# Part B with dense projections, its heads moved to 32-row groups through DRAM, and its instructions in an order laid down by hand

## The chip, the cores and the metric

The kernel runs on one core of one Trainium2 chip, in one launch. The metric is the device time of a run in microseconds; the time before is the median of three runs.

## What is computed

`x` has 2048 tokens of width 640. Part A is a recurrent attention over 64 segments of 32 tokens with 8 memory rows carried from segment to segment; the change does not touch its code. Part B is an attention of 32 heads of 20 numbers each, in which a token looks at itself and seven earlier tokens two apart. A gate mixes both.

```python
def _B_ref(x, wqkv, wo):
    B, S, D = x.shape
    H = 32
    Dh = D // H
    W, dil = (8, 2)
...
    logits = jnp.einsum('bhsd,bhswd->bhsw', q, kg) * scale
    logits = jnp.where(mask[None, None, :, :], logits, -1000000000.0)
    attn = _softmax(logits, axis=-1)
    o = jnp.einsum('bhsw,bhswd->bhsd', attn, vg)
    return (lambda x, *d: x.transpose(*d))(o, 0, 2, 1, 3).reshape(B, S, D) @ wo
x = A_x
g = _sigmoid((x * gate_w).sum(-1, keepdims=True))
a = _A_ref(x, A_mem0, A_Wq, A_Wk, A_Wv, A_Wo, A_seg_len)
b = _B_ref(x, B_wqkv, B_wo)
return g * a + (1 - g) * b
```

## The kernel before

The program has three stages in time. **Part B** (`part_b`, L90 to L331) computes the gate and all of Part B, writes (1 - g) * b to a DRAM scratch, and stores x, transposed, for Part A. **The prepass** (`prepass`, L422) projects the last 8 tokens of every segment with Part A's Q, K and V weights. **Part A** (`part_a`, L519) runs the 64 segments.

Part A's weights are cut into 80 slices of 384 KB (`slice_keys`, L333). 14 are streamed again in every segment, the others stay in SBUF. Of those, N_EARLY = 23 are loaded while Part B runs, and with them the 20 slices of Part A's output weight are copied within DRAM into a contiguous scratch, `wscr` (`load_early`, L377). Another 27 are loaded when Part B's SBUF is given back (`load_late(0)`), and 16 later.

Part B works on five blocks of tokens: four of 484 (`BQ` = 4 x 121) and one of 112. In a block the queries are split by parity of the position into units of 121 (`nu` = 4 of them), so that a unit's eight keys lie in a band of 128 consecutive rows. `steps` (L292) lists (block b, group g of 4 heads), 8 groups a block. The weights of Q, K and the output are padded: every head of 20 columns stands in 32 (`wqk`, L125; `wop`, L124), so a group of 4 heads fills 128 rows and each head starts at a multiple of 32, where the small matmuls of `scores` and `values` need it. The padding costs memsets on POOL and copies on DVE and POOL at the start (L130, L135, L138).

For each step the code calls, in this order, `proj` of the next step (L219: 2 chains of 5 matmuls, one for Q and one for K, with DVE copying Q and ACT copying K out of PSUM), `scores` (L234: 16 matmuls, two exponentials on ACT, two multiplications by the band mask on DVE), `values` of the step before (L256: 16 matmuls for the sums, 16 for the outputs, then logarithm and exponential on ACT for the reciprocal, L271 and L272, and the normalization on DVE, L274), and, from block 1 on, one `out_tile` (L277: 2 chains of 8 matmuls on 128 tokens, scaled by ACT and DVE, stored from ACT's queue). Once a block there are `make_xT` (L159: 20 transposes, the gate, the copies to `xh_blk` on POOL and their store) at g = 2 and `make_v` (L201: 8 chains of 5 matmuls) at g = 6. The order on each engine in Part B is chosen by the scheduler from this program order and its estimates; nothing is fixed by hand there. In Part A the order on PE, ACT and DVE is written by hand (L556).

PSUM has 8 banks: two for all chains (`psm`, L108), four for scores (`psS`, two tiles of two banks), one each for outputs and sums (`psO`).

DMAs of weights, of `xh_blk` and of small things go on SP's queue, those of x and of the outputs on ACT's. Two `issue_after` edges fix an order on SP: `load_early` and the streamed loads of the prepass come after the first store of `xh_blk` (L297, L916).

## Time and profile before

| what | us |
|---|---|
| median of three runs | 1759.74 (1759.62 to 1760.73) |
| the profiled execution's own time | 1748.09 |
| its span, first to last instruction | 1746.1 |
| Part B, to the prepass's first matmul | 0 to 225.4 |
| prepass, to Part A's first matmul | 225.4 to 385.5 |
| Part A | 385.5 to 1746.0 |

Over the span PE is busy 95%, ACT 50%, DVE 37%, POOL 4%. DMA moves 466.5 MB. The granted TensorE clock is 0.998. The profile's chain of waits lists what ended last, step by step; a busy share is an average over three stages that have different limits, so the stages are read one by one. The time of one execution lies between the first and the last instruction's marks, its span, plus about 2 us around it.

### The profile page before, as it was taken

The page shows a single profiled execution, that of the slowest core. Times are in us where ns is not written, and L with a number is a line of the kernel's source. Part 1 is how long each engine was busy: PE and PEld are TensorE (multiplying, and loading weights), DVE is VectorE, ACT ScalarE, POOL GpSimd, SP SyncE. Part 2 cuts the span into 40 slices and gives each one's busy share as a digit, 9 for nine tenths or more (in the row PEclk, how much of TensorE's full clock was granted, in tenths as well). Part 3 has the DMA queues.
Part 4 walks back from the last instruction along what each step waited for, and adds up shares of the span by engine and source line. Part 5 has one row for each costly group of instructions (what it writes and reads, how often), then busy time and mean ns, then how long its engine had stood idle before and what let it go on. Part 6 is the DMA issues. An engine that isn't in the chain of part 4 may idle for free.

```text
span 1746.1 us, 82407 instructions
## 1 busy us (share of the span) xinstructions
PE 1666.4 (95%) x36527; PEld 994.9 (57%) x36527; DVE 649.4 (37%) x2065; ACT 868.5 (50%) x2377; POOL 69.9 (4%) x132
## 2 busy tenths in 40 slices
PE   6899999999999999999999999999999999999989
PEld 3555544445556555556555555555555555555557
DVE  4565533223333333333333333333333333333330
ACT  3776632224555555555555555555555545555550
POOL 4011000000000000000000000000000000000000
PEclk9999999999999999999999999999999999999999
DMA  6951184899999999999999999999999989999981
GB/s 172 335 133 27 42 303 113 221 275 309 307 299 304 298 309 299 305 301 308 295 302 302 299 300 300 302 298 307 303 297 305 298 295 300 306 302 298 300 288 30
DMA packets 280648, 466.50 MB, mean 267 GB/s; under 512 B 94820, under 2 KB 155748, under 8 KB 280292
## 3 DMA queue, kind: packets, MB, share of 16 engines
q1 hardware_dynamic: 178632, 401.83, 69.6%
q10 hardware_dynamic: 101660, 59.41, 11.7%
q8 instruction: 285, 4.67, 1.1%
q14 instruction: 71, 0.58, 0.1%
HBM read 427.47 MB, written 41.55 MB: 269 GB/s over the span
## 4 chain that ended last, share of the span: by engine, by line
PE 86%; ACT 7%; issue 2%; DMA 2%; DVE 2%; ACTq 1%; DVEq 0%
PE ps_qk L569 26%; PE ps_v L662 13%; PE ps_wo L726 12%; PE ps_qkT L586 6%; PE ps_pre L442 6%; PE ps_S L616 5%; PE ps_oT L685 3%; PE ps_z L883 3%; PE ps_bqk L226 3%; ACT bP L249 2%; PE ps_pre L454 2%; ACT ZB L810 2%; PE ps_mem L736 1%; PE ps_bv L213 1%; PE ps_S L625 1%
## 5 line engine op out<-in xcount | busy, mean ns | idle before, releaser
L578 ACT CAST TZ<-ps_qk 128x384 bf16<-128x384 f32 x448 | 208.2, 479 | 326.2 <-PE ps_qk L569 180.4
L569 PEld LDWEIGHTS <-hT 128*32 128x32 bf16 x10240 | 246.5, 96 | 150.0 <-DVE hT L739 13.2
L593 DVE COPY ZB<-ps_qkT 128x384 bf16<-128x384 bf16 x256 | 91.6, 358 | 377.6 <-PE ps_qkT L586 211.7
L569 PE MATMUL ps_qk<-wres_q,hT 128*32 128x384 bf16 x4096 | 225.8, 327 | 1.8 <-issue 1.5
L662 PE MATMUL ps_v<-wlate_v,hT 128*32 128x384 bf16 x4096 | 224.6, 329 | 0.0
L726 PEld LDWEIGHTS <-TZ 128*32 128x32 bf16 x6144 | 153.6, 96 | 65.8 <-issue 18.0
L569 PE MATMUL ps_qk<-wlate_k,hT 128*32 128x384 bf16 x2560 | 159.7, 328 | 0.0
L569 PE MATMUL ps_qk<-wst,hT 128*32 128x384 bf16 x1792 | 153.2, 328 | 0.3 <-issue 0.2
L662 PEld LDWEIGHTS <-hT 128*32 128x32 bf16 x5120 | 113.6, 96 | 68.9 <-issue 6.2
L726 PE MATMUL ps_wo<-wlate_oa,TZ 128*32 128x384 bf16 x2560 | 139.2, 327 | 2.3 <-issue 2.3
L616 PE MATMUL ps_S<-ZB,TZ 128*128 128x160 bf16 (+1 forms) x1024 | 136.9, 238 | 0.4 <-issue 0.4
L586 PE MATMUL ps_qkT<-ident,TZ 128*128 128x128 bf16 x1536 | 130.2, 221 | 0.2 <-issue 0.2
L726 PE MATMUL ps_wo<-wlate_ob,TZ 128*32 128x256 bf16 x2688 | 123.2, 275 | 7.4 <-issue 7.3
L586 PEld LDWEIGHTS <-TZ 128*128 128x128 bf16 x1536 | 89.1, 98 | 61.3 <-issue 40.8
L569 PE MATMUL ps_qk<-wres_k,hT 128*32 128x384 bf16 x1792 | 120.3, 328 | 1.2 <-issue 0.6
L634 ACT ACTIVATE ZB<-ps_S 32x224 bf16<-32x224 f32 x256 | 89.0, 348 | 41.7 <-PE ps_S L625 38.1
L696 DVE CAST TZ<-ps_oT 128x192 bf16<-128x192 f32 x256 | 79.4, 351 | 63.6 <-PE ps_oT L690 63.6
L696 ACT CAST TZ<-ps_oT 128x192 bf16<-128x192 f32 x256 | 69.7, 327 | 57.7 <-PE ps_oT L690 57.7
L616 PEld LDWEIGHTS <-TZ 128*128 128x128 bf16 (+1 forms) x1024 | 58.9, 95 | 68.4 <-issue 41.0
L739 DVE CAST hT<-ps_mem 128x24 bf16<-128x24 f32 x126 | 22.6, 179 | 195.7 <-PE ps_mem L736 195.7
L669 ACT CAST TZ<-ps_v 128x384 bf16<-128x384 f32 x192 | 92.3, 481 | 3.2
L546 POOL COPY TZ<-ZB 128x384 bf16<-128x384 bf16 x64 | 32.5, 507 | 1495.9 <-DMA ZB<-zpk_dram 582.5
(142 smaller groups left out, 2431.2 us busy)
## 6 DMA issues: line engine op xcount, KB each, us to landing
wst<-in_A_Wq_dram SPq DMA_DIRECT2D x260, 384.0 KB
wst<-in_A_Wv_dram SPq DMA_DIRECT2D x260, 384.0 KB
wst<-in_A_Wk_dram SPq DMA_DIRECT2D x195, 384.0 KB
wst<-wscr SPq DMA_DIRECT2D x192, 384.0 KB
zpk_dram<-ZS ACTq DMA_DIRECT2D x4, 3072.0 KB
ZB<-zpk_dram ACTq DMA_DIRECT2D x64, 192.0 KB
wscr<-in_A_Wo_dram SPq DMA_DIRECT2D x20, 384.0 KB
wres_q<-in_A_Wq_dram SPq DMA_DIRECT2D x16, 384.0 KB
```

What stands on the lines that cost most here:

```text
L226: nc.tensor.matmul(ps[:, 0:nn], lhsT=wqk[n][:, kc, 4 * g:4 * g + 4, :].rearrange("p h d -> p (h d)"), rhs=xT[:, kc, o0:o0 + nn], start=(kc ...
L442: nc.tensor.matmul(ps[:], lhsT=sls[r][kc][:, c0:c0 + 128], rhs=zTi[:, kc, :], start=(kc == 0), stop=(kc == KC - 1))
L569: nc.tensor.matmul(pq[32 * j:32 * j + 32, 0:384], lhsT=hT[:, kc, :], rhs=sl[:, 384 * j:384 * j + 384], start=(kc == 0), stop=(kc == KC - 1 ...
L578: cp(sts[i], pqs[i][:, 0:384])
L586: nc.tensor.transpose(pT[:, t, :, :, :].rearrange("p j b i -> p (j b i)"), st[:, 128 * t:128 * t + 128], self.ident[:])
L593: nc.vector.tensor_copy(q_blocks(R)[:, 1:5, :, :].rearrange("p b c i -> p c b i"), pT.rearrange("p t j b i -> p (t j) b i"))
L616: nc.tensor.matmul(grid(h, par)[:, :, 0:80].rearrange("p j (b r i) -> p j b r i", r=2, i=8)[:, :, :, r, :], lhsT=KT[k0:k1, 12 * r + c:12 * ...
L634: nc.scalar.activation(E[ps], pSs[h][ps, :, 112 * j:112 * j + 112], ACT.Exp, scale=scale_a)
L662: nc.tensor.matmul(pvs[R][32 * j:32 * j + 32, 0:384], lhsT=hT[:, kc, :], rhs=sl[:, 384 * j:384 * j + 384], start=(kc == 0), stop=(kc == KC ...
L669: cp(V[R], pvs[R][:, 0:384])
L696: cps[j % 2](oTxs[2 * h + j // 2][:, 6 * (j % 2):6 * (j % 2) + 6, :], pos[j][:, 0:240].rearrange("p (c q) -> p c q", q=40)[:, :, 8:40])
L726: nc.tensor.matmul(pso[part][32 * jj:32 * jj + 32, 0:n], lhsT=oTxs[2 * (R // 2) + j // 2][:, 6 * (j % 2) + 3 * (R % 2) + t, :], rhs=o_weig ...
```

## The change

Part B's work is the same; how it is laid out differs.

- The padded weights go. Q, K and the output weight are loaded as they are (`b_wq`, `b_wk`, `b_wo`), straight into their tiles from SP's and ACT's queues. A projection chunk `f` is 128 dense columns, so a block has 5 chunks for Q and 5 for K in place of 8 groups each. An output tile has 2 chains of 5 matmuls in place of 2 of 8.
- Heads are moved to 32-row groups by DMA. Each chunk of Q and K is copied to SBUF, stored to a DRAM tile (`bqk_dram`) and loaded back half a block at a time, by four DMAs of 20 rows each (`load_qk`). Outputs go the other way: after every fourth group four DMAs of 20 rows store them (`bo_dram`), and one load per block brings them back dense (`load_o`).
- Projections, V and transposes of the next block are spread over the steps of this one, as `jobs`. So are the output chains of earlier blocks.
- All instructions of Part B on PE, ACT, DVE and SP run in the program's order (`manual_schedule`), except the last output tile.
- The early loads are issued two a step from step 0 on, after the step's own transfers; N_EARLY is 21, so two slices move to the late loads. The streamed loads of the prepass come after the load of block 1's outputs (`mid_load`). Output stores move from ACT's queue to SP's.
- In `values` all matmuls of the sums come ahead of those of the outputs.

The core of the diff:

```diff
-N_EARLY = 23
+N_EARLY = 21
...
+            nc.sync.dma_start(wqk[0][:], wsrc[:, :, 0:640])
+            nc.scalar.dma_start(wqk[1][:], wsrc[:, :, 640:1280])
+            nc.sync.dma_start(wv[:], wsrc[:, :, 1280:1920])
...
+            def proj(b, f, n):
...
+                if n == 0:
+                    qk["D"] = wk.tile([128, 2, BQ + HALO], BF, name="bqkD")
+                t = qk["D"]
+                ps = bank(F32, "ps_bqk")
+                for kc in range(KC):
+                    nc.tensor.matmul(ps[:, 0:nn], lhsT=wqk[n][:, kc, 128 * f:128 * f + 128], rhs=xT[:, kc, c0:c0 + nn],
+                                     start=(kc == 0), stop=(kc == KC - 1))
+                self.evac(t[:, n, 0:nn], ps[:, 0:nn], "dve" if n == 0 else "act")
+                if n == 1:
+                    for half in range(2):
+                        r0, r1 = max(128 * f, 320 * half), min(128 * f + 128, 320 * half + 320)
+                        if r0 < r1:
+                            nc.sync.dma_start(qk_dram[b][half, :, r0 - 320 * half:r1 - 320 * half, :].rearrange("n p x -> p n x"),
+                                              t[r0 - 128 * f:r1 - 128 * f, :, 0:nn])
+
+            def load_qk(b, half):
+                nq, nu, c0 = shape_of(b)
+                nn = nq * nu + HALO
+                t = wk.tile([128, 2, 4, BQ + HALO], BF, name="bqkT", bufs=3)
+                src = qk_dram[b][half].rearrange("n (g h d) x -> h d (n g) x", h=4, d=20)
+                for hh in range(4):
+                    nc.sync.dma_start(t[32 * hh:32 * hh + 20, :, :, 0:nn].rearrange("p n g x -> p (n g) x"), src[hh])
+                qk[b, half] = t
...
+            def norm(b, g):
...
+                if g % 4 == 3:
+                    for hh in range(4):
+                        nc.sync.dma_start(heads(ot_dram[b][:])[hh][:, g - 3:g + 1, :], oT[32 * hh:32 * hh + 20, :, 0:nt])
+
+            def load_o(b):
...
+                load = nc.sync.dma_start(OT[:, :, BQ * b:BQ * b + nt], ot_dram[b][:].rearrange("(c p) n -> p c n", p=128))
+                if b == 1:
+                    self.mid_load = load.ins
...
+                for i, (b, g) in enumerate(steps):
+                    nb, jobs = b + 1, []
...
+                    if nb < NB:
+                        nu = shape_of(nb)[1]
+                        if g == 0 and nb < S // 512:
+                            jobs += [lambda kc=kc: xT_chain(nb, kc) for kc in range(KC)] + [lambda: gate(nb)]
+                        chunk = {1: 0, 2: 1, 3: 2, 5: 3, 6: 4}.get(g)
+                        if chunk is not None:
+                            jobs += pj(chunk)
+                        jobs += vu(*[u for u in {1: (0,), 2: (1,), 3: (2,), 4: (3, 4), 7: (5, 6, 7)}.get(g, ()) if u < 2 * nu])
+                    n_out = {0: 1, 4: 2, 5: 1, 6: 1, 7: 2}.get(g, 0) if nb < NB else 2
...
+                    scores(b, g, 0)
+                    scores(b, g, 1)
+                    if prev:
+                        values(*prev)
+                    mask(b, g, 0)
+                    if jobs:
+                        jobs.pop(0)()
+                    mask(b, g, 1)
+                    if prev:
+                        recip(*prev)
+                    if jobs:
+                        jobs.pop(0)()
+                    if prev:
+                        norm(*prev)
+                    for job in jobs:
+                        job()
...
+                    if nb < NB and g == 4:
+                        load_qk(nb, 0)
+                    if nb < NB and g == 7:
+                        load_qk(nb, 1)
+                    if g == 1 and b > 0:
+                        load_o(b - 1)
...
+                    for load in early[:2]:
+                        load()
+                    del early[:2]
...
-        with tc.issue_after(k.first_store):
+        with tc.issue_after(k.mid_load):
             k.prepass()
```

## The prediction

> **What bounds the kernel now.** I read the page's slices first (only the first eighth of the span is Part B), then the stage windows, the chain of waits, the timeline of one step, and last the DMA view, because the change puts new transfers beside old ones. The windows (us, then busy time and instructions of PE, PE's weight loads, DVE, ACT, POOL, then PE clock, DMA share, GB/s):
>
> ```profile
> 0.00:31.40 31.40, 17.62 (x100) 10.09 (x100) 13.12 (x36) 5.49 (x10) 16.41 (x19) 0.95 0.66 184
> 31.40:73.00 41.60, 38.43 (x619) 21.02 (x618) 26.17 (x49) 33.13 (x53) 3.66 (x3) 1.00 0.86 304
> ...
> 161.00:200.00 39.00, 34.94 (x507) 20.20 (x506) 21.68 (x38) 26.36 (x43) 0.00 (x0) 1.00 0.11 39
> 200.00:225.40 25.40, 23.93 (x414) 16.37 (x413) 14.34 (x43) 16.93 (x53) 0.00 (x0) 1.00 0.08 28
> 225.40:385.50 160.10, 156.86 (x732) 70.62 (x732) 48.97 (x72) 41.02 (x72) 0.51 (x1) 1.00 0.78 234
> 385.50:1746.00 1360.50, 1316.31 (x33071) 810.46 (x33071) 475.96 (x1742) 688.68 (x2056) 31.95 (x63) 1.00 0.89 292
> ```
>
> Part B ends at 225.4 us, when the prepass's first matmul starts; the 1520 us behind it are not rewritten. Inside Part B neither PE nor ACT is full. The chain of waits there goes round: projection, ACT's copy of K, two exponentials, logarithm, exponential, output scaling, projection. One such step, from the timeline (start, duration):
>
> ```profile
> 176.21 1.18 PE L226 MATMUL ps_bqk<-xT,wq_pad 128*128 128x484 bf16 x5 [0.75 <-ACT bo L285]
> ...
> 177.23 1.21 PE L226 MATMUL ps_bqk<-xT,wk_pad 128*128 128x498 bf16 x5
> ...
> 178.37 0.43 PE L244 MATMUL ps_bS<-bqT,bkT 32*128 32x121 bf16 x16
> ...
> 178.48 0.57 ACT L77 CAST bkT<-ps_bqk 128x498 bf16<-128x498 f32 x1 [2.32 <-PE ps_bqk L226]
> ...
> 178.95 1.85 ACT L249 ACTIVATE bP<-ps_bS 128x968 bf16<-128x968 f32 x2
> ...
> 179.28 2.35 PE L282 MATMUL ps_bo<-wo_pad,OT 128*128 128x320 bf16 x16
> ...
> 180.67 0.59 ACT L271 ACTIVATE b_rz<-ps_bZ 128x484 f32<-128x484 f32 x1
> ...
> 181.30 0.61 ACT L272 ACTIVATE b_rz<-b_rz 128x484 f32<-128x484 f32 x1
> ...
> 181.81 0.51 ACT L285 ACTIVATE bo<-ps_bo,omg_sb 128x320 bf16<-128x320 f32 x1
> ...
> 182.37 1.18 PE L226 MATMUL ps_bqk<-xT,wq_pad 128*128 128x484 bf16 x5 [0.74 <-ACT bo L285]
> ```
>
> The reader sees a period of 6.16 us in which ACT stood idle for 2.32 us and PE, ahead of each round, for 0.75 us: a loop of latencies, not a full engine.
>
> **What the change takes from PE.** A projection chain of five matmuls takes 1.04 us (176.21 to 177.23, rounded up). Eight groups of 4 padded heads need 16 chains a block, five dense chunks need 10: 6 x 1.04 = 6.2 us a block less. An output tile falls from 16 to 10 matmuls at 2.35/16 = 0.147 us: 0.9 us a tile. Sixteen tiles and four full blocks: about 39 us of PE time less in all, out of a stage that PE does not fill.
>
> **What a block costs in the new order.** ACT, start to start, per step: exponentials 178.95 to 180.67 = 1.72, logarithm 0.63, exponential 0.51, so 2.86; times 8 = 22.9. Beside it, a block: 5 K copies at 0.52 = 2.6, 4 V copies at 0.43 = 1.7, 2.5 xT copies at 0.59 = 1.5, 3.8 output scalings at 0.51 = 1.9, four x loads issued from ACT 1.5, gate 0.2. Sum 32.3. PE: scores 0.36 and values 0.55 a step (178.37 to 179.28), 7.3; 10 projection chains 10.4; 8 V chains at 0.73, 5.8; 7.6 output chains at 0.73, 5.5; transposes and gate 3.1. Sum 32.1. DVE 26. Two engines are nearly level and coupled by two PSUM banks, and step 0 has ACT ahead (5.9 us); I take **34 us a block**, 4.25 a step. Bounds: 32.3 from below, 38 from above (the 42.2 that a block takes now, less the PE time removed).
>
> **Stage by stage, if no transfer is late.** First score: now at 31.4. x has landed at 8.5, five transposes to 11.5, 10 projection chains 10.4, gate 0.6, 8 V chains 5.8: **28**. The first Q/K round trip through DRAM hides behind V: third chunk stored near 18, landing 2.6, half a block of loads 5.0 (below) and 2 more to land. If V did not cover it, 2 us. Three full blocks 102, to 130. Block 3 has no transposes and small projections, ACT 22.9 + 4: 28, to 158. Block 4: ACT rows of that stage 0.35 x 2, 0.25, 0.30, 0.53, with two output chains, 2.1 a step: 17, to 175. There an output tile needs the attention rows of block 3 back from DRAM two steps after they are stored: two landings of 2.6 and transfers of 4 against 4.2 us of cover, so PE, in order, waits 5: 180. At the end block 4's rows make the same trip before the last output tile, and the prepass's first PSUM bank waits for that tile: 8 us, 188 (0 if the scheduler lets the prepass's matmuls go first). That would be 37 us less than 225.4.
>
> **What the transfers add.** This is the step I trust least. The landing of a small store whose reader waits on SP's queue:
>
> ```profile
> SPq L308 <- DMA g_dram<-g_sb: 2.6, 1, 2.6
> ```
>
> The DMA view of three windows (queue: packets, MB, share of 16 engines), first 22 to 28 us, then 50 to 58, then 58.3 to 89:
>
> ```profile
> q1 hardware_dynamic: 1614, 1.09, 86.4%
> ```
> ```profile
> q1 hardware_dynamic: 1169, 3.19, 101.8%
> ```
> ```profile
> q1 hardware_dynamic: 11051, 8.67, 88.6%
> ```
>
> The second window is the resident weights, all engines full: 7 loads in 7.43 us, 1.06 each. The third is the 20 copies of Wo within DRAM: 0.886 x 30.7 = 27 us of all engines, and 39 ns a packet of 784 B. The first is today's only transfer into 20 rows at a time (wo_pad, 608 packets of 1280 B) beside 1006 packets of 320 B of the xh store, 20.5 ns each where that store runs alone (1705 packets, 66.1% of 3.3 us). 0.864 x 96 = 82.9 engine-us, less 20.6, leaves 62.3 for 608: **102 ns** a packet on 10.4 engines at a time, against 55 ns for x's rows of 1280 B into 128 rows.
> The Trainium skill, "SBUF — State Buffer", section "Door 1: The DMA port swizzle", says that a transfer's rate follows the number of 16 ports that its rows reach, and that rows 32 apart share a port. For 20 rows that is 5 ports, by its 27.2 GB/s a port an estimate of 136 GB/s; the slices of 22 to 28 us show 102 to 145. By the page's price the sum below would be 3 us smaller; it also says reading such rows is as slow, which no row shows.
>
> New per block, on the ten engines that carry 20-row transfers: Q/K store, 1280 packets of 996 B, 46 ns (between 39 and 55), 16 engines, 3.7; Q/K load, 1280 packets, 80 ns (102 x 996/1280), 10 engines, 10.2; O store, 640 packets at 78, 10 engines, 5.0 (bounds 2.9, as a 128-row store, and 10, twice; I take the load's price, the nearest row of such a shape); O load 1.8. Already there: x 1.8, xh 2.7, output store 1.7. Sum 27 a block.
> All SP transfers now stand in one order: two early loads a step, 41 in all, over steps 0 to 20. Block 3's first Q/K load stands behind all of them, in step 4 of block 2. Ahead of it lie 20.9 (block 0: no O load or output, half an O store), 27 (block 1), 17.7 (block 2 to there), 21 x 1.06 + 27 = 49.5 early, and 5.3 for five streamed slices of the prepass if they are queued behind the load of block 1's rows: 120. With 2 to land, less 4 of block 0's x and xh that run before step 0 ends, 118 against the 96 us from the end of step 0 to block 3. **22 us of waiting**, since a late Q/K load holds PE's scores, and a late store the copies into the two chunk buffers. Bounds 6 (20-row packets at 46 ns) and 36 (O stores at twice, the loads at 111/102).
> While this holds, PE and ACT have slack: a block of 32 or 38 us instead of 34 changes nothing before block 3.
>
> Two slices moved from early to late: 2 x 1.06 of the prepass's DMA, 0.78 busy; 0 to 2.1 where Part A begins (it waits for a streamed slice at 387 and 392 us); I take 1. POOL loses the padding copies and 8 us of memsets, off the path.
>
> **Sum.** 188 + 22 = 210 against 225.4, plus 1: 14.4 us less. The profiled execution took 1748.1 (span 1746.1); 1733.7 there. The three runs' median is 1759.7, 11.6 above the profiled one, for both kernels alike I assume: **1745**.
>
> **Rivals.** (A) The engines bound it: 20-row packets cost nearly what others do, no wait of note; 188 to 194, 31 to 37 us less, about 1725. For it: DMA's total bytes fit Part B (share 0.11 late in it). Against: the 102 ns. (B) **Slower**: SP's waits on DRAM tiles drain its queue. Three a block (two Q/K loads, one O load), each 2.6 us with nothing running behind it, over 2.6 blocks: 20 us on top of 22, so 230 and 1765; it decides from 15 us on. Against: behind each awaited store stand two early loads of 1.06 to 1.36 us each, about one landing's length. For: where the queue is late, those loads are late too. (C) Part B gets shorter but the prepass and Part A then wait for late weights, and the time comes back: 1757 to 1761. Against: the 27 late loads are now issued by 247 us, and the first of them is read at 291.6.
>
> **Chances.** Forecast (4 to 27 us less) 0.42, A 0.26, B 0.24, C 0.08. Faster by over 0.2% (3.5 us, about what a measurement can tell from no change) 0.65, within it 0.10, slower 0.25. The range leaves out the ends of A and B: 1716 (S near 0, steps at 32.3) to 1770 (B with the dear O stores).
>
> **What would show it.** First score near 28; a step without waits near 4.2 us; ACT's or PE's idle time in blocks 1 and 2 put down to DMA of bqkT (forecast: some 20 us; A: under 6); SP's waits on bqk_dram with a DMA share under 0.7 meanwhile (B); a PE wait of 5 us in block 4; first prepass matmul near 210; Part A's length unchanged to 3 us. Most likely wrong: the price of the 20-row transfers, and how far SP runs ahead.

## The result, and the profile after

The changed kernel takes 1772.38 us (median of 7 runs, 1766.60 to 1776.06), beside it the kernel before 1759.41 us (7 runs): the ratio is 1.0082, with a 95% interval of 1.0059 to 1.0105. It is **slower by 13 us** by the medians (14 by the ratio), where 14 us less had been forecast, and lies above the forecast's range. The profiled execution took 1766.60 us (span 1764.6).

The windows of the changed kernel, cut at the first exponential of each block, at the prepass's first matmul and at Part A's (columns as in the prediction: length, busy time and instructions of PE, its weight loads, DVE, ACT and POOL, then PE clock, DMA share, GB/s):

```profile
0.00:32.95 32.95, 22.25 (x130) 11.87 (x131) 7.35 (x23) 7.35 (x13) 5.08 (x11) 1.00 0.63 182
32.95:69.20 36.25, 31.71 (x492) 17.59 (x491) 21.94 (x41) 27.72 (x43) 3.66 (x3) 0.86 0.91 235
69.20:110.00 40.80, 29.97 (x459) 17.21 (x460) 21.15 (x39) 25.80 (x40) 3.66 (x3) 0.83 0.96 274
110.00:151.00 41.00, 33.66 (x540) 19.87 (x539) 23.99 (x51) 29.20 (x47) 13.95 (x43) 0.88 0.99 266
151.00:192.40 41.40, 32.55 (x615) 20.67 (x614) 25.07 (x48) 32.10 (x53) 0.00 (x0) 0.88 0.57 145
192.40:233.90 41.50, 17.70 (x250) 10.26 (x249) 9.56 (x32) 12.05 (x41) 0.00 (x0) 0.68 0.33 74
233.90:396.60 162.70, 158.09 (x717) 70.99 (x732) 49.04 (x72) 41.35 (x72) 0.51 (x1) 0.99 0.80 240
```

Two of these cuts, 110.0 and 151.0, fall some steps ahead of the first exponentials of blocks 2 and 3, which the records put at 115.9 and 158.5; the first, 32.95, is 0.5 ahead, and Part A's first matmul stands at 395.5, not 396.6 (in the kernel before at 384.5, not 385.5). By exact first exponentials the stretches are: start 33.4, blocks 0 to 2 125.1 (35.8, 46.7, 42.6), block 3 33.9, block 4 with the tail 41.5. Part B ends at 233.9 us, not at 225.4 as before nor at 210 as forecast. The reader is to see three things: the DMA engines are nearly full in blocks 0 to 2, as worked out; in block 4 they are two thirds empty and PE is busy for 17.7 us of 41.5; and the granted clock of PE, 1.00 in all of the old Part B behind the start, is 0.83 to 0.88 in the blocks and 0.68 at the end.

Who waits, in Part B of the changed kernel (engine, tile and line, what it waited for: us in total, times, longest):

```profile
DVE bqkD L79 <- DMA bqk_dram<-bqkD: 22.6, 5, 9.0
...
PE ps_bv L209 <- ACT bqkD L77: 19.2, 4, 8.5
...
PE ps_bo L330 <- DMA OT<-bo_dram: 18.0, 2, 12.6
ACT bqkD L77 <- DMA bqk_dram<-bqkD: 15.1, 4, 7.7
```

The forecast had named both ends of the trip, and looked for the wait at the scores, for `bqkT`. PE's scores wait 1.0 us for it in all. What waits is the other end: the copies into the two chunk buffers, for the store of the chunk before the last. One such wait in the timeline of block 1 (start, length, engine, line, instruction, in brackets the idle time before it and who ended it):

```profile
78.58 0.66 DVE L79 CAST bqkD<-ps_bqk 128x498 bf16<-128x498 f32 x1
...
79.46 0.57 ACT L77 CAST bqkD<-ps_bqk 128x498 bf16<-128x498 f32 x1 [0.61 <-PE ps_bqk L226]
...
80.07 0.43 PE L257 MATMUL ps_bS<-bqkT 20*128 20x121 bf16 x16
...
80.84 1.54 SPq L313 DMA_DIRECT2D bo_dram<-boT  x4
...
83.88 0.43 PE L257 MATMUL ps_bS<-bqkT 20*128 20x121 bf16 x16
83.88 0.39 SPq L185 DMA_DIRECT2D xh_dram<-xh_blk  x1
...
85.14 3.81 SPq L508 DMA_DIRECT2D wres_k<-in_A_Wk_dram  x2
89.08 0.38 SPq L233 DMA_DIRECT2D bqk_dram<-bqkD  x1
...
94.95 0.57 ACT L77 CAST bqkD<-ps_bqk 128x498 bf16<-128x498 f32 x1 [7.68 <-DMA bqk_dram<-bqkD]
94.99 0.68 DVE L79 CAST bqkD<-ps_bqk 128x498 bf16<-128x498 f32 x1 [8.99 <-DMA bqk_dram<-bqkD]
...
95.58 1.49 PE L209 MATMUL ps_bv<-wv_sb,xT 128*128 128x320 bf16 x5 [8.51 <-ACT bqkD L77]
...
98.48 2.85 PE L209 MATMUL ps_bv<-wv_sb,xT 128*128 128x320 bf16 x10
```

From scores to scores, 80.07 to 83.88, a step takes 3.8 us while nothing is late. (The 6.16 us of the step shown of the kernel before are no measure for it: that step held an output tile, this one holds none.) The chunk of 78.58 lies ready at 80.0. SP gets to its store at 89.1, and it lands at 94.9. PE, in order, has V's chain behind the projections and stands for 8.5 us; then it runs at about half speed, 1.49 us for five matmuls that took 0.84 at 79.30. The end of Part B, SP first and then PE:

```profile
195.00 2.22 SPq L242 DMA_DIRECT2D bqkT<-bqk_dram  x4
...
197.65 0.43 SPq L508 DMA_DIRECT2D wst<-in_A_Wk_dram  x1
199.07 1.01 SPq L375 DMA_DIRECT2D hT<-in_A_mem_dram  x2
200.19 1.43 SPq L337 DMA_DIRECT2D bsc_dram<-bo  x1
201.72 1.76 SPq L313 DMA_DIRECT2D bo_dram<-boT  x4
203.52 2.54 SPq L375 DMA_DIRECT2D hT<-in_A_mem_dram  x3
...
206.85 0.37 SPq L318 DMA_DIRECT2D OT<-bo_dram  x1
```
```profile
211.37 2.85 PE L330 MATMUL ps_bo<-b_wo,OT 128*128 128x320 bf16 x10 [12.55 <-DMA OT<-bo_dram]
...
215.22 1.53 PE L330 MATMUL ps_bo<-b_wo,OT 128*128 128x320 bf16 x10
...
230.29 2.85 PE L330 MATMUL ps_bo<-b_wo,OT 128*128 128x320 bf16 x10 [5.49 <-DMA OT<-bo_dram]
```

Block 3's last outputs were ready at 194.8. Their stores are issued at 201.7, behind the loads of block 4's `bqkT`, loads for Part A and an output store; their load is issued at 206.9, behind more loads for Part A, and lands at 211.4. Of these 16.6 us, the two stretches with loads for Part A (197.3 to 200.1 and 203.5 to 206.1) are 5.4.

### The profile page after: what moved, and what is told of

Read it like the earlier page. It is cut to its first block, busy times and chain, and to the rows that moved or that the text cites. A ratio compares the mean times of both kernels' runs of the same rounds, so it can differ in the third digit from the quotient of the medians.

```text
span 1764.6 us, 82095 instructions
## 1 busy us (share of the span) xinstructions
PE 1646.6 (93%) x36266; PEld 980.1 (56%) x36281; DVE 634.1 (36%) x2045; ACT 864.6 (49%) x2362; POOL 58.8 (3%) x124
## 4 chain that ended last, share of the span: by engine, by line
PE 85%; DMA 5%; ACT 4%; issue 3%; SPq 1%; DVE 1%; ACTq 1%; DVEq 0%
PE ps_qk L680 25%; PE ps_v L773 13%; PE ps_wo L837 12%; PE ps_pre L553 6%; PE ps_qkT L697 6%; PE ps_S L727 5%; PE ps_z L994 3%; PE ps_oT L796 3%; PE ps_pre L565 2%; ACT ZB L921 2%; PE ps_bqk L226 1%; DMA bqk_dram<-bqkD 1%; PE ps_bv L209 1%; PE ps_mem L847 1%; PE ps_S L736 1%
## 5 line engine op out<-in xcount | busy, mean ns | idle before, releaser
L680 PE MATMUL ps_qk<-wres_q,hT 128*32 128x384 bf16 x4096 | 225.4, 327 | 1.9 <-issue 1.2
L680 PE MATMUL ps_qk<-wlate_k,hT 128*32 128x384 bf16 x3072 | 180.6, 328 | 0.0
L697 PEld LDWEIGHTS <-TZ 128*128 128x128 bf16 x1536 | 89.2, 98 | 61.1 <-issue 40.6
L745 ACT ACTIVATE ZB<-ps_S 32x224 bf16<-32x224 f32 x256 | 89.0, 348 | 42.3 <-PE ps_S L736 38.4
L773 PE MATMUL ps_v<-wst,hT 128*32 128x384 bf16 x1024 | 87.1, 330 | 5.9 <-DMA wst<-in_A_Wv_dram 5.9
L680 PE MATMUL ps_qk<-wres_k,hT 128*32 128x384 bf16 x1280 | 88.0, 328 | 2.2 <-issue 1.8
```

Source lines behind the costliest of these rows:

```text
L680: nc.tensor.matmul(pq[32 * j:32 * j + 32, 0:384], lhsT=hT[:, kc, :], rhs=sl[:, 384 * j:384 * j + 384], start=(kc == 0), stop=(kc == KC - 1 ...
L697: nc.tensor.transpose(pT[:, t, :, :, :].rearrange("p j b i -> p (j b i)"), st[:, 128 * t:128 * t + 128], self.ident[:])
L745: nc.scalar.activation(E[ps], pSs[h][ps, :, 112 * j:112 * j + 112], ACT.Exp, scale=scale_a)
L773: nc.tensor.matmul(pvs[R][32 * j:32 * j + 32, 0:384], lhsT=hT[:, kc, :], rhs=sl[:, 384 * j:384 * j + 384], start=(kc == 0), stop=(kc == KC ...
```

## The experiments

Theories on trial. **Q**: transfers stand behind the early loads and behind each other, in SP's order and on the DMA engines. **R**: the trip through DRAM (store, landing, load) is too long whatever stands beside it. **T**: the same for the trip of Q and K alone. **C**: two chunk buffers are too few. **F**: SP's order of issue alone; against it **B**: the DMA engines are full, so that a store lands late wherever it is issued. **P**: the 20-row form. And for the end, **the orders of SP and of PE there** against the trip itself. (e12 has two theories of its own, which it calls C and D.) The kernels are read by the same stretches throughout; times in us, each from one profiled execution, the ratio to the kernel before from repeated runs:

| kernel | first score | blocks 0-2 | block 3 | block 4, tail | Part B's end | Part A's start | ratio, 95% interval |
|---|---|---|---|---|---|---|---|
| before | 32.0 | 131.3 | 40.6 | 21.6 | 225.4 | 384.5 | 1 |
| changed | 33.4 | 125.1 | 33.9 | 41.5 | 233.9 | 395.5 | 1.0082 [1.0059, 1.0105] |
| e1_chunk4 | 33.0 | 121.9 | 31.0 | 46.4 | 232.4 | 391.9 | 0.9999 [0.9974, 1.0023] |
| e2_early1 | 31.7 | 115.8 | 35.8 | 53.0 | 236.3 | 395.7 | 1.0053 [1.0023, 1.0083] |
| e3_tail | 33.0 | 124.1 | 33.6 | 31.5 | 222.2 | 381.5 | 0.9971 [0.9951, 0.9992] |
| e4_all | 32.3 | 109.7 | 42.0 | 36.7 | 220.7 | 379.5 | 0.9958 [0.9936, 0.9980] |
| e5_noearly | 32.5 | 108.8 | 31.2 | 43.1 | 215.6 | 389.5 | 1.0024 [1.0003, 1.0044] |
| e6_rows128 | 32.1 | 116.5 | 31.1 | 43.2 | 222.9 | 382.3 | 0.9989 [0.9971, 1.0007] |
| e7_gpq | 42.8 | 198.6 | 54.8 | 53.7 | 349.8 | 509.1 | 1.0720 [1.0684, 1.0756] |
| e8_gpq_tail | 42.9 | 200.5 | 57.2 | 49.2 | 349.7 | 511.0 | 1.0690 [1.0655, 1.0725] |
| e9_actq | 33.5 | 135.0 | 35.7 | 42.3 | 246.4 | 407.6 | 1.0161 [1.0105, 1.0217] |
| e10_actq_tail | 32.9 | 139.9 | 40.1 | 31.0 | 243.9 | 403.2 | 1.0109 [1.0077, 1.0141] |
| e11_actq_all | 32.8 | 134.5 | 37.2 | 31.5 | 236.0 | 395.5 | 1.0096 [1.0062, 1.0130] |
| e12_fill | 31.7 | 126.1 | 34.6 | 33.9 | 226.3 | 385.0 | 0.9979 [0.9955, 1.0004] |
| e13_prevqk | 32.2 | 127.2 | 31.6 | 46.5 | 237.6 | 399.1 | 1.0050 [1.0027, 1.0072] |
| e14_prevqk_noearly | 32.9 | 109.7 | 31.3 | 38.6 | 212.5 | 384.7 | 1.0006 [0.9982, 1.0030] |
| e15_chunk4_tail | 31.6 | 120.7 | 33.7 | 31.7 | 217.7 | 377.2 | 0.9950 [0.9931, 0.9969] |
| e16_defer | 31.6 | 111.3 | 36.0 | 56.3 | 235.2 | 396.2 | 1.0033 [1.0008, 1.0058] |
| e17_defer_outs | 31.0 | 108.6 | 35.7 | 32.4 | 207.8 | 367.0 | 0.9914 [0.9881, 0.9947] |
| e18_defer5 | 32.1 | 112.9 | 39.9 | 33.0 | 217.9 | 377.2 | 0.9944 [0.9918, 0.9971] |

Two things are read from the table as a whole. How far one execution stands for a kernel: blocks 0 to 2 of the changed kernel, e3, e12 and e13, in which no edit moved them, lie between 124.1 and 127.2, so 3 us there mean nothing. And what Part A's start moves, the ratio moves too, to 8 us (changed +11.1 and 0.0082 x 1759 = +14.4; e7 +124.6 and +127; e17 -17.5 and -15.1). Part A itself, whose code is the same in all, takes 1361.4 to 1378.5 us in these executions, in no order with the edits: 1361.7 before, 1369.1 changed, 1369.6 in e17, the fastest. Executions of one kernel differ by as much (the kernel before: 1749.47 to 1769.73 us in one series). So the 7.4 us by which Part A is longer in the profiled pair are not shown to be the change's. (The first four expectations take 118 us for blocks 0 to 2, by the cuts of the windows above; by first exponentials it is 125.1.)

### e1_chunk4: four chunk buffers

```diff
-                    qk["D"] = wk.tile([128, 2, BQ + HALO], BF, name="bqkD")
+                    qk["D"] = wk.tile([128, 2, BQ + HALO], BF, name="bqkD", bufs=4)
-N_EARLY = 21
+N_EARLY = 20
```

> The changed kernel with four buffers for the Q/K chunks (bqkD) in place of two; one resident slice fewer is loaded early (N_EARLY 20) to make room. Theory Q (SP's queue is late because the DMA engines are full of early loads and 20-row transfers): DVE's and ACT's waits for bqk_dram (22.6 and 15.1 us) go, but the wait moves to the loads of bqkT; Part B ends within 4 us of the changed kernel's 233.9. Theory C (two chunk buffers are too few; DMA itself has time enough): the 24 us that the chain of waits spends on bqk_dram go for the most part; Part B ends at 212 to 220 and the median falls by 14 to 22 us.

Blocks 0 to 2 fell by 3.2 us, by itself no more than the spread; but the same edit gives 3.4 us beside e3 (e15), 5.4 beside e10 (e11), and e4, with e3's edit too, lies 6.1 below e2. So four buffers are worth some 3 to 6 us. The landing of the chunk stores went from 10.3% of Part B's chain to 3.5%, while PE's wait for OT rose from 18.0 to 25.7 us: most of the wait moved, as Q has it. The total, though, fell by 15 us, to the kernel before's, as C has it, where Part A's start moved by 3.6 us only. The changed kernel was profiled in its fastest execution (1766.60, median 1772.38) and e1 in its second slowest (1763.28, median 1757.42), so that the stages understate the gain; where the rest of it arose is not shown.

### e2_early1: one early load a step

```diff
-                    for load in early[:2]:
+                    for load in early[:1]:
-                    del early[:2]
+                    del early[:1]
```

> The changed kernel with one early load a step in place of two, so that the 41 of them are spread over all 40 steps. Theory Q: the demand of blocks 0 to 2 falls by some 22 us of full DMA engines, so blocks 0, 1 and 2 together fall from 118 us to 96 to 104, and blocks 3 and 4 rise by up to 8 (they had room: DMA share 0.57 and 0.33); Part B ends at 218 to 226. Theory C: the chunk store still waits its turn on SP behind landings; blocks 0 to 2 stay above 112.

Blocks 0 to 2 fell by 9.3 us, under the 14 to 22 of theory Q. Block 4 grew by 11.5, since early loads now reach into it and the outputs' trip stands behind them.

### e3_tail: the order of the queue at the end

```diff
-                misc.append(load_first)
+                first = [load_first]
...
+                misc = misc[:1] + first + misc[1:]
...
-                    n_out = {0: 1, 4: 2, 5: 1, 6: 1, 7: 2}.get(g, 0) if nb < NB else 2
+                    n_out = {0: 1, 4: 2, 5: 1, 6: 1, 7: 2}.get(g, 0) if nb < NB else (2, 2, 0, 0, 0, 1, 1, 1)[g]
...
-                    if b >= 3:
+                    if (b, g) >= (2, 5):
```

> The changed kernel with two orders changed near the end: the small loads (gate values, first rows of Part A) are issued from step 5 of block 2 on, the rows of Part A first, and the output chains of block 3's rows are not called in steps 2 to 4 of block 4 (2, 2, 0, 0, 0, 1, 1, 1 chains a step, the rest after the last step). Both theories: blocks 0 to 2 as they were (118 us). If the 12.6 us for which PE waits for OT in block 4, and the stores that are late behind small loads in block 3, are the order of SP's queue and of PE: block 3 falls from 41.4 to 34 to 38, the stage from block 4 to the prepass from 41.5 to 26 to 31, Part B ends at 216 to 224, and the median falls by 10 to 18 us. If they are the price of the round trip itself: that stage stays above 37.

The loads for Part A now go out from block 2 on, and output chains that need block 3 come later. Block 4 with its tail fell from 41.5 to 31.5 us, and the total to 1751.74, ratio 0.9971: this edit alone takes the kernel below the one before. The changed kernels without it have 38.6 to 53.7 us there; those with it, where no early load stands at the end and GpSimd issues nothing, 31.0 to 33.9. The two orders together are shown as the cause. How much is whose was not run apart; the rows say some. In e3:

```profile
200.05 0.39 SPq L318 DMA_DIRECT2D OT<-bo_dram  x1
...
204.33 1.51 PE L330 MATMUL ps_bo<-b_wo,OT 128*128 128x320 bf16 x5 [4.51 <-DMA OT<-bo_dram]
```

Counted from block 4's first exponential (192.4 and 190.7), OT lands after 13.6 us in place of 19.0: SP's order gave 5.4. The rest of the 10 us goes with the output chains that were kept back: they fill PE's later waits, and of the second wait for OT, 5.49 us at 230.29 in the changed kernel, nothing is left.

### e4_all: e1, e2 and e3 together

> All three together: four chunk buffers, one early load a step, and the order of the end. If Q and C each hold in part and the end is an order: Part B ends at 190 to 205 (start 33, blocks of 30 to 34, end 27 to 30), so some 20 to 35 us before the kernel before the change, and the median is near 1730. If the waits only move: above 215.

Blocks 0 to 2 fell to 109.7, but block 3 rose to 42.0: the early loads, now one a step, run on beside block 3's and block 4's outputs. Part B ended at 220.7, not at 190 to 205; the waits moved.

### e5_noearly: no early load beside the steps

```diff
-                    for load in early[:2]:
+                    for load in early[:0]:
-                    del early[:2]
+                    del early[:0]
```

> None of the 41 early weight loads is issued beside Part B's steps; they are all issued after the last step, so the stage behind Part B waits for them, and the total is expected to rise whatever the theory. Read are the three blocks from the first exponential of block 0 to that of block 3, 125.1 us in the changed kernel. Theory Q (the early loads are what the small transfers stand behind, on SyncE's queue and on the DMA engines): these blocks fall to 93 to 102 us, the waits of the chunk copies for their stores fall from 22.6 and 15.1 us to under 5 each, and the granted clock in these blocks rises from 0.83 to 0.88 to over 0.93. Theory R (the trip through DRAM and SyncE's order of small transfers are too long by themselves): the blocks stay above 112 us, with waits for bqkT or the chunk stores of 10 us and more.

Blocks 0 to 2 took 108.8 us, between the theories: R had over 112, Q 93 to 102. The waits of the chunk copies fell, as Q has it, in all of Part B to these, and in blocks 0 to 2 to 0.5 us:

```profile
DVE bqkD L79 <- DMA bqk_dram<-bqkD: 6.7, 4, 2.5
...
ACT bqkD L77 <- DMA bqk_dram<-bqkD: 1.2, 1, 1.2
```

But the blocks without them are 36.3 us each, and the DMA share is down:

```profile
32.50:65.90 33.40, 29.67 (x493) 16.89 (x497) 21.60 (x41) 27.08 (x44) 4.16 (x3) 0.90 0.65 158
65.90:103.20 37.30, 33.85 (x553) 19.77 (x556) 24.41 (x47) 30.09 (x49) 4.17 (x3) 0.91 0.61 148
```

So the early loads, two in a step, cost some 16 us there, and what remains is the steps' own length. Block 0, in which no output chain runs yet, takes 33.4 us; blocks 1 and 2, with output chains, 37.3 and 38.1. (With four buffers and one early load in a step, e4, e16 and e17 are as short: 108.6 to 111.3.) All 41 loads behind Part B made the prepass 12 us longer (173.8 against 161.7).

### e6_rows128: bqkT in 128 rows

```diff
-                src = qk_dram[b][half].rearrange("n (g h d) x -> h d (n g) x", h=4, d=20)
-                for hh in range(4):
-                    nc.sync.dma_start(t[32 * hh:32 * hh + 20, :, :, 0:nn].rearrange("p n g x -> p (n g) x"), src[hh])
+                for n in range(2):
+                    src = qk_dram[b][half, n]
+                    src = bass.AP(tensor=src.tensor, offset=src.offset, ap=[[nn, 128], [64 * nn, 4], [1, nn]])
+                    nc.sync.dma_start(t[:, n, :, 0:nn], src)
```

> Q and K of a block half come back from DRAM by two transfers of 128 rows, in place of four of 20 rows. The rows that are read are not those of the heads: the arrangement of Q and K into head groups is left out, and the same tiles are filled with as many columns. Theory P (the 20-row form keeps the DMA engines busy longest, as the prediction priced it: some 80 ns for a packet of 1 KB): the bytes rise by 1.6, the packets of these loads too, but they are spread over all engines, and the blocks 0 to 2 fall by 13 to 18 us from 125.1. Theory Q (the place in SyncE's order and the early loads decide): they change by less than 5 us, either way.

116.5: 8.6 us less, between P's 13 to 18 and Q's under 5. The form has a price, some half of what P took, though the edit also halves the number of issues on SP (two for four), which is not told apart. The forecast's price for a packet itself holds. The DMA view of the changed kernel from 160.5 to 166 us:

```profile
q1 hardware_dynamic: 831, 0.97, 75.6%
```

That is 0.756 x 16 x 5.5 = 66.5 us of engines for 831 packets, 80 ns each. By the trace's packet records, 600 of them are the 996-byte packets of `bqkT` and take 75 ns on average, where 80 had been taken; 116 are packets of 3 KB of a weight slice, at 163 ns.

### e7_gpq and e8_gpq_tail: the small transfers from GpSimd

```diff
-                            nc.sync.dma_start(qk_dram[b]
+                            nc.gpsimd.dma_start(qk_dram[b]
...
-                    nc.sync.dma_start(t[32 * hh
+                    nc.gpsimd.dma_start(t[32 * hh
...
-                        nc.sync.dma_start(heads(ot_dram
+                        nc.gpsimd.dma_start(heads(ot_dram
```

e8 has e3's edit as well.

> The stores of the Q and K chunks, the loads of bqkT and the stores of O are issued by GpSimd, which has next to nothing else to do in Part B, in place of SyncE; the early loads and the loads of OT stay on SyncE. Bytes and packets stay the same. Theory F (SyncE's issuing in order is the cause: a store whose data is ready stands behind loads that wait for something else): the blocks 0 to 2 fall from 125.1 to 95 to 108 us, the waits of the chunk copies for their stores from 38 us in sum to under 12, and block 4 with its tail from 41.5 to some 34. Theory B (the DMA engines' share of time, 0.91 to 0.99 in these blocks, is the cause): the blocks stay above 117 us.

> The edit of e7_gpq and that of e3_tail together. Theory F: blocks 0 to 2 at 95 to 108 us, block 3 at 31 to 34, block 4 with its tail at 26 to 31.5, so the first matmul of the stage behind Part B at 187 to 207 us, and the total 15 to 30 us below that of e3_tail (1751.74 us). Theory B: only the tail's gain stays, the first matmul of the next stage at 215 to 225 us, and the total within 5 us of e3_tail's.

Both are over 120 us slower than the kernel before, and tell nothing of F against B: GpSimd itself is slow to issue. In e7's waits (the idle time ahead of an issue, total, times, longest):

```profile
POOL bqkT L242 <- issue: 65.0, 22, 4.3
...
POOL bqk_dram L233 <- issue: 47.8, 14, 8.1
```

Some 3 us ahead of a transfer, four transfers to a half block, one after another.

### e9_actq, e10_actq_tail, e11_actq_all: chunk stores from ScalarE's queue

```diff
-                            nc.sync.dma_start(qk_dram[b]
+                            nc.scalar.dma_start(qk_dram[b]
```

e10 adds e3's edit, e11 e3's and the four buffers of e1.

> Only the stores of the Q and K chunks change their issuer: ScalarE's queue, right behind its own copy of the chunk, in place of SyncE's. GpSimd as the issuer took some 3 us for each transfer (65.0 us of issue over 22 loads of bqkT), so that e7_gpq could not tell the theories apart; ScalarE already issues the loads of x. Theory F (SyncE's order of issue makes the chunk stores late): the waits of the chunk copies for these stores, 38 us in the changed kernel, fall under 10, and the blocks 0 to 2 from 125.1 us to 104 to 114. Theory B (the DMA engines are full, so that a store lands late wherever it is issued): they stay above 119 us, with the same waits or with waits for bqkT in their place. Either way the block 4 with its tail stays within 3 us of 41.5, since nothing of it is changed.

> The edit of e9_actq with that of e3_tail. Theory F: blocks 0 to 2 at 104 to 114 us, block 4 with its tail at 30 to 34, the first matmul of the next stage at 202 to 214 us, and the total 8 to 18 us below e3_tail's 1751.74. Theory B: within 4 us of e3_tail.

> e10_actq_tail with four buffers for a Q and K chunk in place of two (and one early load fewer, to make room). Theory F: the chunk buffers are no longer waited for once their stores are issued in time, so that this gives under 3 us against e10_actq_tail. Theory B: four buffers cover a store that lands late, and the blocks 0 to 2 are 3 to 8 us shorter than in e10_actq_tail.

F falls. The stores go out at once and the copies' waits for them are small, but blocks 0 to 2 are longer, 134.5 to 139.9 us. SP's waits in e9, and its issues beside ScalarE's in block 1:

```profile
SPq L242 <- DMA bqk_dram<-bqkD: 35.5, 5, 21.2
...
SPq L313 <- DMA bqk_dram<-bqkD: 15.5, 4, 5.7
```
```profile
86.11 0.38 ACTq L233 DMA_DIRECT2D bqk_dram<-bqkD  x1
```
```profile
85.67 7.03 SPq L313 DMA_DIRECT2D bo_dram<-boT  x4
92.80 0.39 SPq L185 DMA_DIRECT2D xh_dram<-xh_blk  x1
93.23 3.13 SPq L508 DMA_DIRECT2D wres_k<-in_A_Wk_dram  x2
96.52 0.38 SPq L318 DMA_DIRECT2D OT<-bo_dram  x1
```

The store issued at 86.11 landed at 92.4, 6.3 us later, with early loads on the engines. SP's four O stores, which read nothing of it, took 7.03 us to issue and were released by that landing; the load of OT came 11 us after the first of them, and PE waited 23.3 us for OT in blocks 0 to 3, where it had waited 19.2 for V's place behind the copies. With the store off SP's queue the landing is as late, and the wait turns up on SP and at OT in its place, dearer here. Why SP stands for a landing that its transfer does not read, the trace does not say. The four buffers of e11 gave 5.4 us in blocks 0 to 2, as B has it.

### e12_fill: matmuls that keep PE from standing

```diff
+            def fill(chains):
+                for _ in range(chains):
+                    ps = bank(F32, "ps_fill")
+                    for c in range(KC):
+                        nc.tensor.matmul(ps[:, 0:320], lhsT=xT[:, c, HALO:HALO + 128], rhs=wo[:, c, 0:320],
+                                         start=(c == 0), stop=(c == KC - 1))
...
+                    if b == 4:
+                        fill(2)
...
                 load_o(NB - 1)
+                fill(6)
```

> e3_tail with matmuls that compute nothing that is used: ten at the end of each step of block 4, and thirty behind the last values, while PE stands for the trips of O. Theory C (the granted clock, 0.67 in block 4 of e3_tail, falls because PE stands, and it costs time there): the clock of the stretch rises over 0.85, a chain of five output matmuls falls from 1.46 us to 0.7 to 0.9, and block 4 with its tail falls from 31.5 to 27 to 30 us. Theory D (the clock falls with the waits, but the trips through DRAM alone set the time): it stays at 31 to 35 us, whatever the clock.

The window of block 4 with its tail:

```profile
192.40:226.30 33.90, 30.81 (x375) 19.55 (x375) 10.53 (x33) 12.64 (x41) 0.00 (x0) 0.95 0.35 101
```

The clock rose from 0.67 to 0.95 and a chain of five fell from 1.46 us to between 0.76 and 0.85 in most places: the clock falls because PE stands. The stretch did not get shorter (33.9 against 31.5). That fits D, but the filler itself is 27.6% of that stretch's chain, so what the clock costs at the end is not settled by it.

### e13_prevqk and e14_prevqk_noearly: no dependence on the chunks

```diff
-                src = qk_dram[b][half].rearrange("n (g h d) x -> h d (n g) x", h=4, d=20)
+                src = qk_dram[max(b - 1, 0)][half, :, :, 0:nn].rearrange("n (g h d) x -> h d (n g) x", h=4, d=20)
```

e14 has e5's edit as well.

> From block 1 on, Q and K are read back from the DRAM tile of the block before: the scores use the wrong block's Q and K, the transfers, bytes and packets stay, and only the dependence of these loads on the landing of this block's chunks is gone. Theory T (the trip, store to landing to load, holds up SyncE and the scores): the blocks 0 to 2 fall from 125.1 us to 108 to 117. Theory B (the transfers themselves stand in the DMA engines and the chunk buffers come free late): they stay above 120 us.

> The edits of e13_prevqk and e5_noearly together: no early load beside Part B, and no dependence of bqkT on the chunks. This is the length of the steps themselves. If the prediction's 34 us for a block without waits is right, the blocks 0 to 2 take 100 to 104 us; if the steps are longer than it took, with PE's lower clock or more work on the path, they stay within 3 us of e5_noearly's 108.8.

Without the dependence blocks 0 to 2 are as long as with it (127.2 and 125.1; 109.7 and 108.8 without early loads). T falls: it is not the trip of Q and K. And a block with neither is 36.5 us long, not 34. In e14's block 1 the chain runs through ACT, transposes and gate first, and then PE:

```profile
71.89 0.59 PE ps_g L173 x16
...
73.96 4.08 PE ps_bqk L226 x10
...
79.64 2.21 PE ps_bqk L226 x10
```

Step 0 takes until 74.0, 7.2 us, and the first pair of projection chains behind it 4.08 us in place of 2.21. The steps of this block, by first exponentials, are 6.5, 5.8, 3.8, 4.7, 4.2, 3.9, 3.7 and 4.9 us. The dear pair is PE's clock. The same block, cut where the clock changes:

```profile
66.80:70.90 4.10, 2.17 (x52) 1.53 (x44) 2.98 (x7) 3.85 (x6) 0.00 (x0) 1.00 0.70 141
70.90:77.70 6.80, 6.37 (x82) 3.35 (x80) 3.37 (x9) 3.59 (x6) 4.17 (x3) 0.50 0.55 151
77.70:104.30 26.60, 25.49 (x424) 14.78 (x426) 17.95 (x34) 22.61 (x36) 0.00 (x0) 1.00 0.56 146
```

During the transposes, between which PE pauses for copies by up to 1.04 us, PE is busy for half of the time; then its clock stands at 0.50 for 6.8 us. One such stretch lies in each of blocks 0 to 2 of e5 and e14. The scores, sums, outputs and the pair of projection chains take 5.55 us in it (72.48 to 78.03), and the same rows a step later 3.13 (78.71 to 81.84): 2.4 us, on the chain.

### e15 to e18: clearing both ends at once

e15_chunk4_tail is e1 and e3 together. The other three add to it:

```diff
-                    for load in early[:2]:
+                    for load in early[:1 if b < 3 else 0]:
-                    del early[:2]
+                    del early[:1 if b < 3 else 0]
```
```diff
-                for load in early + misc:
+                for load in misc:
                     load()
                 for job in outs:
                     job()
+                for load in early:
+                    load()
```

e16_defer has the first of these, e17_defer_outs both, e18_defer5 both with `1 + i % 2` in place of `1`.

> The edits of e1_chunk4 and e3_tail together, the early loads left at two in a step. If their gains add, blocks 0 to 2 take 120 to 123 us, block 3 some 31, block 4 with its tail some 31.5, the next stage's first matmul comes at 215 to 219 us (e3_tail 222.2), and the total is 3 to 7 us below e3_tail's ratio of 0.9971. If the waits only move, its first matmul stays at 221 to 226 us.

> As e15_chunk4_tail, but with one early load in each step of blocks 0 to 2 and none in blocks 3 and 4; the 16 or so that are left are issued behind the last step. If early loads and small transfers only stand in each other's way, blocks 0 to 2 take about 110 us (e4_all 109.7), block 3 some 31, block 4 with its tail 31 to 32, the next stage's first matmul comes at 203 to 208 us, and that stage is 4 to 7 us longer (e5_noearly, which put all 41 there, 14.8): the total 6 to 12 us below e4_all's 0.9958. If the loads put off cost as much as they gave, the total stays within 3 us of e4_all's.

> e16_defer with the 16 early loads that are put off issued behind the last output chains, so that these chains' stores no longer stand behind them. Blocks 0 to 3 as in e16_defer (147 us from the first score), block 4 with its tail 31 to 33 us in place of 56.3, the next stage's first matmul at 210 to 213 us. If the loads cost time only where they meet the small transfers, that stage is 4 to 7 us longer than 159.5 and the total lands at or below e15_chunk4_tail's ratio of 0.995 (0.992 to 0.996). If they are a fixed cost that comes back, the stage is 10 us longer or more, and the ratio is 0.996 to 1.000.

> As e17_defer_outs, with one and two early loads in turn in the steps of blocks 0 to 2, so that four are put off. Blocks 0 to 2 between e16_defer's 111.3 and e15_chunk4_tail's 120.7 us, block 3 some 32, block 4 with its tail 31 to 33, the next stage's first matmul at 209 to 217 us and that stage within 3 us of 159.5; the ratio 0.991 to 0.995 if the two ends add.

In e15 the gains add: 120.7, 33.7 and 31.7, ratio 0.9950. e16 missed: the 16 loads put off stood on SP ahead of the last output stores, and the end took 56.3 us. With them behind the outputs, e17 has Part B's end at 207.8 and a prepass of 159.2 us, no longer than before's 159.0. The windows of its block 1, block 4 with tail, and prepass:

```profile
63.70:103.30 39.60, 33.23 (x555) 19.54 (x559) 24.45 (x47) 30.30 (x48) 4.17 (x3) 0.96 0.92 241
...
175.40:207.80 32.40, 20.96 (x248) 11.69 (x247) 9.96 (x32) 12.25 (x41) 0.00 (x0) 0.63 0.40 118
207.80:367.00 159.20, 156.21 (x724) 70.25 (x728) 48.07 (x71) 40.10 (x72) 0.51 (x1) 1.00 0.95 286
```

e17 is the fastest kernel of all, 1738.64 us, ratio 0.9914: the change pays with four buffers and with the queue and the last output chains laid out otherwise. (Whether the kernel before would gain from putting off early loads was not run.) The loads are no fixed cost: 16 of them fit into the prepass, whose DMA share rises from 0.80 to 0.95; 41, in e5, did not. e18 shows it is no smooth scale: its block 3 takes 39.9 us, its Part B ends 10 us later than e17's, though only 12 loads more go beside the steps. In that block ACT stands 6.1 us for the landings of output stores (in e17 4.7), and PE 4.6 us for OT (2.1).

## Why the prediction was wrong

**The step that failed** is "Stage by stage, if no transfer is late": 188 us. The same stages, each where the experiments leave it without late transfers, take 31.4 (first score; mean of e15, e16, e17) + 109.2 (blocks 0 to 2; mean of e5 and e14) + 31.2 (block 3; e5, e14) + 31.5 (block 4 with tail; e3) = 203.3 us, or 200.5 without the 2.8 us for which PE still stands in block 3 of e5 and e14 for a chunk's store. That is 12 to 15 us of the 24 by which Part B ended later than forecast; the waits, 31 to 33 us against 22, are the other 9 to 11. The mechanism, transfers that stand in one order and a gain in PE's work that they eat up, was right; the sign was lost by terms that were too small (the start, the blocks, the waits, the end of the tail), and by one that was put at nothing: PE's clock, 1.00 in the old Part B, halves where PE pauses.

- *First score 28*: 33.0 (33.4 by the first exponential). In the chain of the start x lands at 9.9, not 8.5; the first two projection chains take 4.02 us in place of 2.08; 1.9 us are booked to a landing of x ahead of ACT's gate, and 2.55 us to the landing of a chunk's store, with two chunk buffers. The prediction had hidden that trip behind V and forgotten that it holds the buffers as well.
- *34 us a block*: 36.4 (109.2 / 3). It was taken from level engines with 1.04 us a chain. Steps 0 and 1, with the transposes and with PE's clock at 0.50 behind them, are dearer: the clock alone took 2.4 us in e14's block 1, as much as the mean is above 34. No run kept the clock up there. And the mean flatters: blocks 1 and 2, with the output chains that the sum counted, take 37.3 to 38.3.
- *22 us of waiting in blocks 0 to 2*: some 16 (125.1 - 109.2). The share of the DMA engines was about right (0.91 to 0.99), and early loads are its larger part, as summed. But the wait shows at the chunk buffers, and at OT once there are more of them, not at the scores. The price of the 20-row packets holds (75 ns where 80 was taken); the rates of 102 to 145 GB/s that were read from the slices of 22 to 28 us are those of some slices only, the others run up to 256.
- *Block 3, 28*: 33.9. The 31.2 of e5 and e14 still hold PE's wait of 2.8 us for a chunk's store, so that some 28 is right without waits, and the rest is waits.
- *Block 4 and the tail, 17 + 5 + 8 = 30*: 41.5. The last trip, 8, took 9.1 (224.8 to 233.9). The 5 us wait for block 3's outputs was named in the right place, but it is 12.55 us: the sum counted two landings and the transfers, not what SP issues ahead of the O stores and ahead of their load, 5.4 us of it for Part A. With these loads moved and output chains kept back (e3) the stage takes 31.5. Here the prediction broke its own rule of listing what stands ahead on a queue.
- *The slower rival (B)* priced SP's waits on DRAM tiles at 2.6 us each. The waits of SP's `bqkT` loads on `bqk_dram` are 5.0 us in all, and e13 shows that to take that dependence away gives nothing. The outcome was B's, the mechanism was not.
- *Rival A*, with no wait of note, fell: the copies wait 22.6 and 15.1 us for the chunk stores. *Rival C* is not borne out: Part A, forecast unchanged to 3 us, is 7.4 us longer in the profiled pair, within its spread over the kernels, but PE waits 5.9 us for a streamed slice there, against 5.0 before. The prepass took 161.7 us in place of 159.0: PE's clock is still at 0.50 in its first 4.5 us.
- *A step without waits near 4.2 us*: a projection step is shorter, 3.8 us (80.07 to 83.88 in the timeline above); the excess sits in steps 0 and 1.

That the same code with four buffers and another order (e17) ends Part B at 207.8 us, and at 1738.64 us in all, is near the 210 and 1745 of the forecast by luck: its steps are longer and its waits fewer than the forecast had them.

Not settled: what PE's lower clock costs at the end (e12), why SP stands for landings of transfers that it does not read (e9), and where e1 gained the most of its 15 us.

## What to carry to other kernels

When transfers replace compute, write down each queue in its order of issue, with everything on it, up to the last consumer: in the dearest wait here (12.55 us, 4.5 in e3) some 5 us came from loads of 0.3 to 2.5 us that nobody needed yet, ahead of a store and a load that PE needed, and the output chains that could have filled it had run before. Where a buffer waits for a store, more buffers gave a little (3 to 6 us) and another issuer moved the wait. Thinning out the bulk loads among the small transfers removed most of it (one in a step with four buffers was as short as none with two), and the next stage can take the others as long as its DMA share has room. When PE's pauses move, price its clock too: pauses of up to 1 us, with PE busy for half of the time, came ahead of its halving here. Put the loads that are put off behind the last urgent store, not ahead of it.

## What the runs showed of the hardware

PE's granted clock follows its pauses. In the old Part B it is 1.00, and PE's waits in the step shown there are 0.75 us; in the new one 0.83 to 0.88, and 0.68 where PE stands longest. Ten output matmuls take 2.85 us right after a wait of 12.55 us and 1.53 us 4 us later; with filler matmuls the clock of that stretch is 0.95 (e12). The clock records of all these traces know two values, 1.00 and 0.50, and the stretches at 0.50 in Part B last 3.4 us or a multiple of it (6.8 us in each of blocks 0 to 2 of e14, 20.5 at the end of e3). The Trainium skill, "TensorE: Matmul & The Clock Gate", section "Part 1: The HAM clock gate (the "warmup" mystery)", says that the clock is halved after about 3.4 us without work and comes back after about as long of steady work. The halving agrees (2.85 / 1.53 is 1.9), and so does the length of the stretches, the last 3.4 us of which are steady work of PE in the blocks of e14. The 3.4 us without work do not: ahead of the fall at 70.9 in e14 PE was busy for 45% of the last 3.4 us and never paused for more than 1.04.

GpSimd took some 3 us to issue a transfer (65.0 us for 22, e7) where SP's four loads of a half block went out in 1.5 to 2.7 us together in nine of ten cases of the changed kernel. And a chunk store that landed in 2.55 us at the start of the changed kernel took 5.8 us in its block 1 (89.08 to 94.87), beside early loads, and 6.3 in e9's.
